# FNet layer with a gated feed-forward branch: the second sequence chunk of the first DFT changes from plain products to five plain and three seven-product steps, and the weight jobs move

## The chip, the cores and the metric

The program runs on one core of one Trainium2 chip. The metric is device time in microseconds (us) of one execution. Five engines work side by side: TensorE (PE in the profile, with its weight loads as PEld), VectorE (DVE), ScalarE (ACT), GpSimd (POOL) and SyncE (SP). SP issues nearly all DMA transfers of this kernel, one after the other from one queue. Each engine runs its own instructions strictly in the order in which the program holds them.

## The reference

All tensors are float32. S = 2048 tokens, D = 512, F = 1792.

```python
xn = layernorm(x)                                  # over D
a  = einsum("bsd,ed->bse", xn, dft_hid_re)
b  = einsum("bsd,ed->bse", xn, dft_hid_im)
s  = einsum("ts,bse->bte", dft_seq_re, a) - einsum("ts,bse->bte", dft_seq_im, b)
h  = einsum("bsd,df->bsf", xn, w1) + b1
h  = where(h > 0, h, 0) ** 2
g  = silu(einsum("bsf,fd->bsd", h, w2) + b2)
out = x + s * g
```

## The kernel before

Every float32 factor is split into a high part (rounded to TensorE's fp32r format) and a low part (the rest). A product then takes three passes: high by high, high by low, low by high. The high part is made on ACT (`split_hi`, profile line L136), the low part on DVE (`split_lo`, L139), which has to wait for ACT's part.

The largest stage multiplies the sequence DFT matrices by xn. It goes over eight chunks `c` of 256 columns of the DFT (`CW = 256`, `NC = 8`), and in each over eight pairs `j` of x row blocks (`NJ = 8`). A *step* (c, j) is one pair in one chunk. Two ways of multiplying occur:

- *Plain* (chunks 0 and 1 before, `products`, L397): a step takes 24 matmuls of 512 columns.
- *Seven products* (chunks 2 to 7, `mm`, L382): a 2x2 block product with seven instead of eight multiplications. A step takes 7 x 6 = 42 matmuls of 256 columns. It needs sums of the blocks on both sides: of x (`sums` and `split_sums`, `split_s1`, made once while the plain chunks run) and of the DFT columns (`step_sums(n+2)`, three DVE instructions, L304 to L306), and a split of seven blocks into the operand tile `g` (`step_split(n+1)`: ACT L136, then DVE L139, both on 128x1792). There are two `g` tiles in turn, so the split for step n+1 can start when TensorE has left step n-1, and has to be done when it starts step n+1. The DFT columns come as tile `u` (`load_c`, 512 KB, three or four steps ahead).

At the end of a seven-product chunk, seven sums of the seven accumulators make the four output blocks (`closing_of`, L363; ACT first copies some accumulators into tiles `left`). They are handed out over the first steps of the next chunk by the table `LATER = {0: 1, 1: 1, 2: 2, 4: 1}` (step: number of sums); two are made at once. After step max(LATER) the chunk is stored (`pqd<-c`, 1024 KB).

In between, the same engines prepare seven weight blocks for later stages, in *jobs*: `d0` to `d3` (hidden DFT matrices) and `v0`, `v1`, `v6` (three blocks of w1). A job (`weight`) loads a raw block of 512 KB (tile `wd2r` for `d2`, `w10r` for `v0` and so on), for the `d` jobs turns the sign of a part on ACT (L146), makes the sums on DVE (tile `wd2t`), splits first 768 and then 1024 columns (tile `wd2g`), and stores each split to memory (`wdd<-wd2g`, 768 and 1024 KB). It is a generator; the table `EARLY` says after which step which job does its next piece. In this kernel a job has four pieces: load; turn and sums; first split and store; second split and store. All jobs but `d1` share one raw buffer, so a job's load stands behind the previous job's splits.

The order of instructions on each engine is the order in which this Python code emits them; no scheduler moves them. In one turn of the loop over steps the order is: the step's matmuls, `step_sums(n+2)`, `step_split(n+1)`, the load of step n+4, the closing sums, then the pieces that `EARLY` names.

After that stage come the hidden DFT (`YUnit`, L790), the first feed-forward product (`HUnit`, L790) and the second one (`outer`, L896). For the units listed in `ACT_PAIR`, `HUnit` applies relu and square on ACT instead of DVE.

## Time and profile before

| | |
|---|---|
| median of 3 runs | 672.76 us (672.74 to 672.93) |
| the profiled execution's own time | 672.81 us |
| its span, first to last instruction | 671.0 us |
| PE busy | 665.1 us, 99% of the span |
| DVE busy | 596.4 us, 89% |
| ACT busy | 380.2 us, 57% |
| plain chunk 1 on PE (L397) | from 51.1 to 94.8 us |
| seven-product chunks 2 to 7 on PE (L382) | from 94.8 to 323.3 us |

Busy shares are averages over stages. The chain that ended last is PE for 96% of the span, so what counts is whether a stage makes PE wait, and how many columns PE has to stream. A duration of an instruction in the records runs a little into the next one; the distance from start to start is what it occupies its engine.

### The profile page before, as it was taken

To read this page: it belongs to the slowest core of one execution; us is meant where nothing else is said; L and a number is where in the kernel's file an instruction comes from. 1 tells how busy PE (TensorE), PEld (TensorE's weight loads), DVE (VectorE), ACT (ScalarE), POOL (GpSimd) and SP (SyncE) were. 2 spreads that over 40 slices of the span, in tenths; PEclk is the share of its full clock that TensorE was granted. 3 is DMA by queue.
4 is the path that set the end of the run, shared out by engine and by line. 5 is a ranking of instruction groups with operands and counts; after the bars stand their busy time and mean duration, and the time that the engine had idled before them with its cause. 6 is when DMAs were issued, how large, how long until landed. Compare 5 with 4: busy or idle time off the path is not lost.

```text
span 671.0 us, 13184 instructions
## 1 busy us (share of the span) xinstructions
PE 665.1 (99%) x5437; PEld 646.3 (96%) x5437; DVE 596.4 (89%) x831; ACT 380.2 (57%) x524; POOL 8.8 (1%) x11
## 2 busy tenths in 40 slices
PE   9999999999999999999999999999999999999997
PEld 6888889999999999999999999999999999999997
DVE  7997888999999999899899988977877889999997
ACT  6855664634445454444464557888778865454451
POOL 0000000000000000000000000000000000101010
PEclk9999999999999999999999999999999999999999
DMA  8635497646556774759588558565755866777775
GB/s 292 226 115 206 145 347 269 220 142 224 200 167 226 252 282 162 262 186 346 184 303 278 181 189 317 202 251 205 271 182 198 324 243 214 190 218 190 219 205 156
DMA packets 51739, 150.82 MB, mean 225 GB/s; under 512 B 4960, under 2 KB 19552, under 8 KB 50272
## 3 DMA queue, kind: packets, MB, share of 16 engines
q1 hardware_dynamic: 43568, 129.28, 56.9%
q10 hardware_dynamic: 6208, 18.88, 7.1%
q0 software_dynamic: 1904, 1.84, 1.9%
q8 instruction: 42, 0.69, 0.4%
q14 instruction: 17, 0.14, 0.1%
HBM read 101.98 MB, written 47.99 MB: 223 GB/s over the span
## 4 chain that ended last, share of the span: by engine, by line
PE 96%; DVE 1%; ACT 1%; DMA 0%; issue 0%; ACTq 0%; SPq 0%; DVEq 0%
PE m L382 34%; PE m_o L896 15%; PE r_B L790 13%; PE r_A L790 9%; PE pq_b L397 8%; PE r_C L790 4%; PE r_D L790 4%; PE m_last L896 4%; PE pq_ba L397 2%; PE pq_bc L397 2%; PE pq_bb L397 2%; DVE z L1146 0%; DMA x<-in_x 0%; DVE z L946 0%; ACT h L848 0%
## 5 line engine op out<-in xcount | busy, mean ns | idle before, releaser
L382 PEld LDWEIGHTS m<-g,xc 128*128 128x128 f32 x2016 | 228.6, 188 | 0.1
L382 PE MATMUL m<-g,xc 128*128 128x256 f32 x2016 | 228.7, 276 | 0.0
L136 ACT ACTIVATE g<-u 128x1792 fp32r<-128x1792 f32 (+2 forms) x65 | 99.0, 1523 | 126.9 <-PE m L382 89.0
L139 DVE TENSOR_TENSOR g<-u,g 128x1792 fp32r<-128x1792 f32 (+2 forms) x66 | 116.9, 1772 | 19.8 <-ACT g L136 19.2
L896 PE MATMUL m_o<-w,g 128*128 128x256 f32 x882 | 100.5, 276 | 0.0
L896 PEld LDWEIGHTS m_o<-w,g 128*128 128x128 f32 x882 | 100.3, 188 | 0.0
L136 ACT ACTIVATE g<-hr 128x1792 fp32r<-128x1792 f32 (+2 forms) x31 | 48.2, 1565 | 40.0 <-PE m_o L896 16.8
L790 PE MATMUL r_B<-xT,w 128*128 128x256 f32 x504 | 66.6, 277 | 0.4 <-ACT r_B L146 0.4
L397 PE MATMUL pq_b<-g,xc 128*128 128x512 f32 x240 | 65.2, 391 | 0.4 <-DVE small L247 0.4
L790 PEld LDWEIGHTS r_B<-xT,w 128*128 128x128 f32 x504 | 61.5, 188 | 0.5 <-ACT r_B L146 0.5
L139 DVE TENSOR_TENSOR g<-hr,g 128x1792 fp32r<-128x1792 f32 (+2 forms) x31 | 56.7, 1837 | 2.9 <-ACT g L136 2.8
L397 PEld LDWEIGHTS pq_b<-g,xc 128*128 128x128 f32 x240 | 44.7, 188 | 10.7 <-ACT g L136 0.8
L790 PE MATMUL r_A<-xT,w 128*128 128x256 f32 x336 | 42.8, 276 | 0.0
L790 PEld LDWEIGHTS r_A<-xT,w 128*128 128x128 f32 x336 | 40.2, 188 | 0.0
L790 PE MATMUL r_B<-wdp,yg 128*128 128x256 f32 x288 | 35.8, 277 | 0.0
L304 DVE TENSOR_TENSOR u<-u 128x512 f32<-128x512 f32 x48 | 32.8, 684 | 1.9 <-DMA u<-in_ct 1.9
L790 PEld LDWEIGHTS r_B<-wdp,yg 128*128 128x128 f32 x288 | 34.1, 188 | 0.0
L896 PE MATMUL m_last<-w,g 128*128 128x256 f32 x294 | 33.5, 276 | 0.0
L896 PEld LDWEIGHTS m_last<-w,g 128*128 128x128 f32 x294 | 33.4, 188 | 0.0
L139 DVE TENSOR_TENSOR yg<-yraw,yg 128x1792 fp32r<-128x1792 f32 x13 | 26.2, 2018 | 0.6 <-ACT yg L136 0.6
L136 ACT ACTIVATE yg<-yraw 128x1792 fp32r<-128x1792 f32 x13 | 22.2, 1708 | 5.8 <-DVE yraw L313 5.3
L790 PE MATMUL r_D<-xT,w 128*128 128x256 f32 x168 | 23.6, 276 | 0.0
(192 smaller groups left out, 877.8 us busy)
## 6 DMA issues: line engine op xcount, KB each, us to landing
u<-in_ct SPq DMA_DIRECT2D x63, 512.0 KB, 3.8
hd<-h ACTq DMA_DIRECT2D x28, 512.0 KB, 3.9
hr<-hd SPq DMA_DIRECT2D x28, 512.0 KB, 3.8
wdp<-wdd SPq DMA_DIRECT2D x8, 896.0 KB, 6.5
yraw<-pqd SPq DMA_DIRECT2D x13, 512.0 KB, 5.9
pqd<-c SPq DMA_DIRECT2D x6, 1024.0 KB, 6.3
w<-w1d SPq DMA_DIRECT2D x6, 896.0 KB, 8.2
y<-y ACTq DMA_DIRECT2D x8, 512.0 KB, 5.2
```

The lines of the kernel that those rows point to most:

```text
L136: nc.scalar.activation(hi, src, AF.Copy)
L139: nc.vector.tensor_tensor(lo, src, hi.bitcast(F32), op=ALU.subtract)
L304: nc.vector.tensor_tensor(t[:, 0:2], r[:, 0:1].to_broadcast([P, 2, 256]), r[:, 1:3], op=ALU.add)
L382: nc.tensor.matmul(ps[:, d], w[:, a_, d * P:(d + 1) * P], halves(mv(b_)), start=first and d == 0 and (a_, b_) == (HI, HI), stop=last and ( ...
L397: nc.tensor.matmul(accs[c][k], w, part[c, j][:, b_, 2 * h:2 * h + 2], start=j == 0 and h == 0 and (a_, b_) == (HI, HI), stop=j == NJ - 1 a ...
L790: nc.tensor.matmul(self.region(REGION[k]), w, mv, start=i == 0 and k in (1, 7), stop=i == len(ops) - 1, skip_group_check=True)
L896: nc.tensor.matmul(m[:, i * 256:(i + 1) * 256], ready[n][:, a_, H_SLOT[a], i * P:(i + 1) * P], W2[p][:, b_, b], start=p == 0 and i == 0 an ...
```

## The change

Chunk 1 is now multiplied in two ways. Five x pairs (`MIXED = 4, 5, 6, 7, 2`) are multiplied plainly, in matmuls of 256 columns, into four accumulators (`plain_step`); three of those accumulators are the ones that products 2, 3 and 4 of the seven use, the fourth is called Z. Then three pairs (`SEVEN = 1, 0, 3`) are multiplied by seven products into the same accumulators. The closing of chunk 1 therefore goes through `closing_of`, with one more DVE sum for Z. The sums of x no longer have a separate buffer for S1 (`split_s1` is gone; `split_sums` splits four blocks at once), and two of the eight `split_sums` come after the first seven-product step.

A weight job has five pieces instead of four: its first sum stands apart from the other two. `EARLY` is rewritten: `d0` begins in the plain steps and ends in the three seven-product steps, `d1` to `v6` follow in chunks 2 to 6 (`d1` used to be made in chunk 1 with a buffer of its own, and `d2` was begun there). In five places the last piece of a job and the load of the next job stand together, and the next job's second piece one step later. `LATER` hands out one closing sum per step. `ACT_PAIR` loses unit 5.

```diff
-PLAIN = 2
-SIDE = {7: 1}
+MIXED = 4, 5, 6, 7, 2
+SEVEN = 1, 0, 3
...
 EARLY = {
-    (2, 0): ("d2",), (2, 1): ("d2",), (2, 2): ("d3",), (2, 4): ("d3",), (2, 5): ("d3",), (2, 6): ("d3",),
-    (3, 1): ("v0",), (3, 3): ("v0",), (3, 5): ("v0",), (3, 6): ("v0",),
...
+    (1, 0): ("d0",), (1, 3): ("d0", "d1"), (2, 1): ("d1",), (2, 2): ("d1",), (2, 3): ("d1",), (2, 5): ("d1", "d2"),
+    (2, 6): ("d2",), (2, 7): ("d2",), (3, 1): ("d2",), (3, 3): ("d2", "d3"), (3, 4): ("d3",), (3, 5): ("d3",),
...
-LATER = {0: 1, 1: 1, 2: 2, 4: 1}
+LATER = {0: 1, 1: 1, 2: 1, 3: 1, 4: 1}
+LATER_1 = {0: 1, 1: 1, 2: 1, 3: 1, 4: 1, 5: 1}
...
-ACT_PAIR = (4, 5, 6, 8, 10, 12, 14, 16, 18, 21, 25)
+ACT_PAIR = (4, 6, 8, 10, 12, 14, 16, 18, 21, 25)
...
+    def plain_step(j):
+        g = part.pop((1, j))
+        for k, pairs_ in ((2, ((A11, 1), (A12, 3))), (4, ((A21, 1), (A22, 3))), (3, ((A11, 0), (A12, 2))),
+                          (Z, ((A21, 0), (A22, 2)))):
...
+            for i, (a, q) in enumerate(pairs_):
+                mm(ms[k], XC[j][:, a], lambda b_: g[:, b_, q], ...)
...
-    steps = [(c, j) for c in range(PLAIN, NC) for j in range(NJ)]
+    steps = [(1, j) for j in SEVEN] + [(c, j) for c in range(2, NC) for j in range(NJ)]
...
-    def weight(n, raw_, sums_, to, k, e=None, turn=False):
+    def weight(n, raw_, sums_, to, k, turn=False):
...
-        sums_(t, r)
+        first = sums_(t, r)
+        next(first)
+        yield
+        list(first)
         yield
...
+        if n == 0:
+            split_sums(2)
+            split_sums(7)
```

How the order of instructions moves, at two places. Numbers behind a name tell instances apart (`g3_0` is the operand of step (3, 0), `u3_1` the columns of step (3, 1), `wd1g` the split weights of job `d1`).

SP, the queue of DMA issues, around the load of one raw weight block. Before, at the load for `d3`:

```order
L432 DMA wdd2_85<-wd2g_939 256x1x768
L293 DMA u2_5_991<-in_ct 128x1024
L432 DMA wdd2_85<-wd2g_939 256x1x1024
L293 DMA u2_6_1044<-in_ct 128x1024
L423 DMA wd3r_1046<-in_wd 128x1024
L293 DMA u2_7_1097<-in_ct 128x1024
```

Now, at the load for `d2`, after step (2, 5):

```order
L286 DMA u3_1_1361<-in_ct 128x1024
L660 DMA pqd1_76<-c1_916 128x2048
L450 DMA wdd1_84<-wd1g_1253 256x1x1024
L438 DMA wd2r_1368<-in_wd 128x1024
L286 DMA u3_2_1419<-in_ct 128x1024
```

The raw block's load stood one step behind the last store of the job before, with a column load between; now it stands directly behind that store and, here, behind the store of a whole chunk.

DVE, after step (2, 5). Before, with the job `d3` at its sums and first split:

```order
L304 TENSOR_TENSOR wd3t_1047<-wd3r_1046 128x512
L305 TENSOR_TENSOR wd3t_1047<-wd3t_1047,wd3r_1046 128x256
L306 TENSOR_TENSOR wd3t_1047<-wd3t_1047,wd3r_1046 128x256
L304 TENSOR_TENSOR u2_7_1097<-u2_7_1097 128x512
L305 TENSOR_TENSOR u2_7_1097<-u2_7_1097 128x256
L306 TENSOR_TENSOR u2_7_1097<-u2_7_1097 128x256
L139 TENSOR_TENSOR g2_6_1203<-u2_6_1044,g2_6_1203 128x1792
L139 TENSOR_TENSOR wd3g_1208<-wd3r_1046,wd3g_1208 128x768
```

Now:

```order
L139 TENSOR_TENSOR g2_6_1358<-u2_6_1197,g2_6_1358 128x1792
L373 TENSOR_TENSOR c1_916<-m4_1_580,c1_916 128x2x256
L139 TENSOR_TENSOR wd1g_1253<-wd1t_1036,wd1g_1253 128x1024
L300 TENSOR_TENSOR u3_0_1305<-u3_0_1305 128x512
L302 TENSOR_TENSOR u3_0_1305<-u3_0_1305 128x256
L303 TENSOR_TENSOR u3_0_1305<-u3_0_1305 128x256
L139 TENSOR_TENSOR g2_7_1416<-u2_7_1250,g2_7_1416 128x1792
L300 TENSOR_TENSOR wd2t_1369<-wd2r_1368 128x512
L300 TENSOR_TENSOR u3_1_1361<-u3_1_1361 128x512
L302 TENSOR_TENSOR u3_1_1361<-u3_1_1361 128x256
L303 TENSOR_TENSOR u3_1_1361<-u3_1_1361 128x256
L139 TENSOR_TENSOR g3_0_1468<-u3_0_1305,g3_0_1468 128x1792
```

Between the end of one job (`wd1g`) and the first sum of the next (`wd2t`), which needs the load above, one column sum and one `g` split are left. On ACT the sign turn of `wd2r` stands between the high parts of `g2_7` and `g3_0` in the same way.

## Prediction

> **What bounds the kernel now.** First the page's engine rows and the clock row, then the chain of waits and the busy time by stage.

> ```profile
> PE 665.1 (99%) x5437; PEld 646.3 (96%) x5437; DVE 596.4 (89%) x831; ACT 380.2 (57%) x524; POOL 8.8 (1%) x11
> PEclk9999999999999999999999999999999999999999
> ```

> TensorE (PE) is busy all the time at full clock. Two things can change the total: the number of columns PE streams, and idle time that PE does not have today. The chain's pieces price a column:

> ```profile
> 56.56 2.04 PE pq_b L397 x9
> 58.60 0.68 PE pq_ba L397 x3
> ...
> 94.13 0.70 PE pq_ba L397 x3
> 94.83 228.49 PE m L382 x2016
> ```

> A 512-column matmul of plain chunk 1 takes 2.04 / 9 = 0.2267 us, a 256-column one of the seven products 228.49 / 2016 = 0.11334 us: half, to the nanosecond. Shorter matmuls cost nothing extra. A seven-product step is 42 x 0.11334 = 4.76 us; chunk 2's steps start at 94.83, 99.59, 104.35 and so on.

> By stage (columns: sum, busy time of PE, PEld, DVE, ACT, POOL, clock, DMA share, GB/s):

> ```profile
> 51.10:94.80 43.70, 43.70 (x195) 36.03 (x194) 36.84 (x47) 25.62 (x37) 0.00 (x0) 1.00 0.63 230
> 94.80:132.90 38.10, 38.10 (x339) 38.10 (x338) 34.55 (x44) 20.29 (x18) 0.00 (x0) 1.00 0.70 247
> 132.90:171.00 38.10, 38.10 (x339) 38.10 (x338) 35.40 (x45) 17.61 (x14) 0.00 (x0) 1.00 0.57 202
> ```

> PE never waits here, but in chunks 2 and 3 DVE is busy 34.6 and 35.4 of 38.1 us. So the question is how far DVE runs ahead of PE.

> **How much room a step has.** The timeline of ACT, then DVE, in chunk 2 (start, duration):

> ```profile
> 99.69 1.71 ACT L136 ACTIVATE g<-u 128x1792 fp32r<-128x1792 f32 x1 [1.79 <-issue]
> 115.58 0.61 ACT L146 ACTIVATE wd3r<-wd3r 128x512 f32<-128x512 f32 x1
> ...
> 101.43 2.03 DVE L139 TENSOR_TENSOR g<-u,g 128x1792 fp32r<-128x1792 f32 x1 [0.30 <-ACT g L136]
> 103.37 1.22 DVE L139 TENSOR_TENSOR wd2g<-wd2t,wd2g 128x1024 fp32r<-128x1024 f32 x1
> 104.51 0.69 DVE L304 TENSOR_TENSOR u<-u 128x512 f32<-128x512 f32 x1
> 105.23 0.42 DVE L305 TENSOR_TENSOR u<-u 128x256 f32<-128x256 f32 x1
> 105.69 0.43 DVE L306 TENSOR_TENSOR u<-u 128x256 f32<-128x256 f32 x1
> 106.19 2.02 DVE L139 TENSOR_TENSOR g<-u,g 128x1792 fp32r<-128x1792 f32 x1
> ...
> 194.03 0.68 DVE L363 TENSOR_TENSOR c<-m,c 128x512 f32<-128x512 f32 x1
> 194.63 0.68 DVE L304 TENSOR_TENSOR u<-u 128x512 f32<-128x512 f32 x1
> ```

> PE starts a step at 99.59. ACT's high part starts 0.10 later, DVE's low part at +1.84, and it ends at +3.87, while PE needs it at +4.76 (its first matmul, 0.11 us, takes the high parts alone). So DVE can be late by 1.0 us and no more. From start to start a low part occupies DVE 1.94 us, a closing sum 0.60, the 1024-column weight split 1.14, three column sums 1.52 (0.72, 0.46, and 0.43 less an overlap of 0.09).

> **The change, part by part.**

> *Columns.* A plain step keeps its columns (24 x 512 = 48 x 256); in three steps 48 matmuls become 42. Saved: 3 x 6 x 0.11334 = **2.04 us**. Chunk 1 also ran 43.72 us (51.11 to 94.83) against 192 x 0.2267 = 43.53, slower only near its end (the 0.70 row): 0.19 more. The shorter ACT_PAIR takes work off ACT in the feed-forward units, where PE has this one wait for ACT; at most it gives all of it back, at least nothing:

> ```profile
> PE r_B L790 <- ACT r_B L146: 0.4, 1, 0.4
> ```

> Together −2.6 us.

> *DVE in the three seven-product steps.* In steps (1, 1) and (1, 0) DVE has, between two low parts, two `split_sums` of 1024 columns (1.14 each, like the weight split) and three column sums: 1.14 + 1.14 + 1.52 + 1.94 = 5.74 against 4.76. At the turn to chunk 2 it has two closing sums, a 1024-column weight split and three column sums: 1.20 + 1.14 + 1.52 + 1.94 = 5.80, and the split has to wait for ACT. Followed through the order row by row, DVE enters step (1, 1) with its margin spent on the plain steps' work, and each of the three excesses falls on PE: 0.96 us each, **+2.9 us**. Bounds: if it enters with its 1.0 us of margin and ACT costs nothing, 1.9; if ACT's part of a split, 1.71 us for the largest, comes wholly in the way once, 4.6.

> *The weight loads: the large term.* Five times (after (2, 5), (3, 3), (4, 0), (4, 5), (5, 3)) the next raw block is loaded right behind the previous job's last store, and its sums are due one step later; before, two steps lay between. Let T be PE's start of step (2, 5). DVE's low part of g(2, 6) runs T+1.84 to T+3.78, then a closing sum to T+4.38, then the weight split, which ends at T+5.60. Only then SP issues the store, and 0.5 us later the load, at about T+6.15. On ACT the sign turn stands before the high part of g(3, 0); on DVE the first sum stands before that low part. PE needs g(3, 0) at T + 3 x 4.76 + 0.11 = T+14.39. After the landing come the turn 0.61, the first sum 0.60 (512 columns, like a closing sum), three column sums 1.52, the low part 2.02: 4.75 us. So the block may land at T+9.64, **3.5 us after its issue**; for `v` jobs, which have no turn, 4.1 us. All later time is idle time of PE, one for one.

> How long do such loads take? Issues of the trace (KB each, us from issue to landing; first all seven raw loads, then the stores of 1024 KB):

> ```profile
> wd0r<-in_wd SPq DMA_DIRECT2D x1, 512.0 KB, 4.6
> wd1rt<-in_wd SPq DMA_DIRECT2D x1, 512.0 KB, 5.4
> wd2r<-in_wd SPq DMA_DIRECT2D x1, 512.0 KB, 4.9
> wd3r<-in_wd SPq DMA_DIRECT2D x1, 512.0 KB, 4.8
> w10r<-in_w SPq DMA_DIRECT2D x1, 512.0 KB, 4.3
> w11r<-in_w SPq DMA_DIRECT2D x1, 512.0 KB, 4.6
> w16r<-in_w SPq DMA_DIRECT2D x1, 512.0 KB, 5.6
> ...
> wdd<-wd1g SPq DMA_DIRECT2D x1, 1024.0 KB, 4.7
> wdd<-wd3g SPq DMA_DIRECT2D x1, 1024.0 KB, 6.8
> w1d<-w10g SPq DMA_DIRECT2D x1, 1024.0 KB, 5.4
> pqd<-c SPq DMA_DIRECT2D x6, 1024.0 KB, 6.3
> u<-in_ct SPq DMA_DIRECT2D x1, 512.0 KB, 9.1
> ```

> None of the seven landed within 4.1 us, though no store stood right ahead of any. The last row is the `u` issued at 80.74, behind a load pair and two weight stores begun at 77.99:

> ```profile
> 77.99 0.33 SPq L423 DMA_DIRECT2D wd2r<-in_wd  x1
> 80.74 0.56 SPq L293 DMA_DIRECT2D u<-in_ct  x1
> 80.00:90.00 10.00, 10.00 (x45) 8.26 (x44) 8.30 (x15) 4.70 (x7) 0.00 (x0) 1.00 1.00 371
> ```

> It waited its turn behind all of them: 512 + 512 + 768 + 1024 + 512 = 3328 KB from 77.99 to 89.84, 11.85 us, with the DMA engines full at 371 GB/s. From this:

> - After (3, 3), (4, 0), (5, 3): a 1024 KB store directly ahead. It lands 4.7 to 6.8 us after its issue, say 5.8; the load is issued 0.5 later and needs 512 KB at 371 GB/s, 1.4 us, more: 6.7 us. PE idles 6.7 − 3.5 = 3.2, then 2.6 and 2.6: **8.4 us**.
> - After (2, 5), (4, 5): column load, chunk store, weight store, raw load, 3072 KB within about 2.2 us. By the measured case 11.85 x 3072 / 3328 = 10.9 after the first issue, 8.7 after the load's own. PE idles 5.2 and 4.6; and in the step after it DVE has two closing sums, the two remaining weight sums (0.80, like the two column sums from 105.23), column sums and low part: 1.20 + 0.80 + 1.52 + 1.94 = 5.46 against 4.76, 0.7 more each time: **11.2 us**.

> Bounds of the five: if the store ahead costs nothing and each lands in the median 4.8 us, 1.3 + 0.7 + 0.7 + 2.0 + 1.4 = 6.1; if the store takes its longest 6.8 and the 9.1 us of the full queue holds with 1 us on top, about 25. I take 19.6: the queue of issues is the same as in the measured row.

> Nothing after chunk 6 moves enough to count: the last job ends at (6, 0), its copies are read chunks later.

> **Sum.** −2.6 + 2.9 + 19.6 = +19.9. The profiled execution took 672.81 (span 671.0 and 1.8 around it), 0.05 above the median of 672.76; the forecast is 692.7 us, **slower by 3%**.

> **Rivals.** Under 0.2% (1.35 us) no measurement of this kernel tells a difference.

> 1. *Loads land as quickly as before.* If stores and loads share the engines so that the load does not wait for the store, the five cost 6.1 as bounded above: 672.8 − 2.6 + 2.9 + 6.1 = 679. For it: `wd2r` landed in 4.9 us with 2816 KB issued behind it. Against it: the 9.1 us row, where the late one paid. Chance 0.14.
> 2. *Faster.* The one point that decides is whether the raw blocks land within 3.5 and 4.1 us. Then the five waits vanish; with 1.9 for the DVE excess it would end at 672.1, with the excess hidden in DVE's margin too at 670.2. Column loads do land that fast, but none of the seven raw loads did:

> ```profile
> u<-in_ct SPq DMA_DIRECT2D x63, 512.0 KB, 3.8
> ```

> Chance 0.02 for faster, 0.03 for no change.
> 3. *PE loses its clock in the long waits.* The two longest waits leave PE idle for 4 to 5 us at a stretch. A slow start shows what a lower rate costs:

> ```profile
> 1.22 5.46 PE L503 MATMUL warm<-idle 128*128 128x512 bf16 x13 [1.22 <-DVE idle L499]
> ```

> 13 warm-up matmuls took 0.42 us each, where warm ones take 0.227. One such stretch loses 13 x 0.193 = 2.5 us; after two long waits 5.0, so 697.7. DVE would catch up meanwhile, so this is an upper price. [...] Chance 0.13, since the idle time is cut by matmuls on the high parts alone.

> The rest, 0.68, is the forecast with its own range of 687 to 698. The range of 684 to 700 takes in most of the clock's case and the upper part of the quick loads. Slower 0.95, same 0.03, faster 0.02.

> **What would show it.** On PE, the first product of g(3, 0) (chunk 3's `m`) waiting 4 to 6 us, for ACT or DVE, the same at (5, 0), and 2 to 3 us before (3, 6), (4, 3), (5, 6); ACT's turn of `wd2r` waiting for the DMA `wd2r<-in_wd`, with a landing near 9 us; raw loads at 6 to 10 us where they were 4.3 to 5.6; DVE waits about 1 us short at PE in the steps (1, 0), (1, 3) and (2, 1). Chunk 1 should end near 94.7, no earlier than now by more than 0.5, its saved columns eaten by DVE. The forecast is wrong if those raw loads land in under 4.1 us, or if PE waits mainly in stages after chunk 6.

## The result, and the profile after

The changed kernel takes **705.75 us** (median of 4 runs, 704.02 to 710.22) beside 672.85 us (672.74 to 673.15) for the kernel before: a ratio of 1.050, interval 1.045 to 1.055. It is slower by 33 us. The forecast was 692.7 us with a range of 684 to 700: the sign and the places were right, the size was 13 us too small, and the result lies above the range. The profiled execution took 704.48 us, with a span of 702.7.

The engine rows, the clock row and the first line of the chain, from the page of the changed kernel:

```profile
PE 675.6 (96%) x5611; PEld 662.1 (94%) x5611; DVE 606.6 (86%) x841; ACT 380.6 (54%) x516; POOL 8.8 (1%) x11
PEclk9999999989999999999999999999999999999999
PE 69%; DVE 18%; DMA 7%; ACT 3%; issue 1%; SPq 1%; ACTq 0%; DVEq 0%
```

The chain was 96% PE before. Now it leaves PE for DVE, DMA and ACT, and one slice of the clock row shows less than full speed. The waits of PE say where (us in total, times, longest):

```profile
PE m L388 <- DVE g L139: 14.8, 8, 3.9
PE m L388 <- ACT c L146: 4.3, 1, 4.3
...
PE r_B L799 <- ACT r_B L146: 1.2, 1, 1.2
```

By stage (the columns are those of the table of before: length, busy time of PE, PEld, DVE, ACT, POOL, clock, DMA share, GB/s), cut at the ends of chunk 1, of step (2, 6), of step (5, 7) and of chunk 7:

```profile
50.93:94.69 43.76, 42.57 (x367) 42.08 (x366) 37.35 (x42) 24.63 (x28) 0.00 (x0) 1.00 0.40 138
94.69:129.25 34.56, 33.79 (x296) 33.59 (x295) 32.72 (x42) 15.19 (x12) 0.00 (x0) 1.00 0.60 204
129.25:276.36 147.11, 129.44 (x1052) 127.95 (x1051) 115.22 (x147) 59.76 (x52) 0.00 (x0) 0.94 0.58 204
276.36:353.20 76.84, 76.84 (x676) 76.79 (x675) 66.33 (x82) 33.23 (x27) 0.00 (x0) 1.00 0.70 248
```

Chunk 1 ends at 94.69, where the first product of chunk 2 starts (94.67 before; the 94.83 of the chain of before is the recorded end of chunk 1's last product, which runs a little into the next one): DVE took the saved columns back. The third row is where the time went: 25 steps of 4.76 us make 119.0 us, and they took 147.11, with a mean clock of 0.94. Chunk 7 ends at 353.20, 29.9 us later than before, and what follows it takes 349.5 us against 347.7.

That the raw blocks are what is waited for is seen in the timeline of ACT and DVE ahead of step (3, 0) (the bracket is the idle time before, and what ended it):

```profile
135.76 0.63 ACT L146 ACTIVATE wd2r<-wd2r 128x512 f32<-128x512 f32 x1 [9.31 <-DMA wd2r<-in_wd]
...
136.42 0.69 DVE L300 TENSOR_TENSOR wd2t<-wd2r 128x512 f32<-128x512 f32 x1 [7.49 <-ACT wd2r L146]
```

The DMA issues of the five blocks (KB, us from issue to landing):

```profile
wd2r<-in_wd SPq DMA_DIRECT2D x1, 512.0 KB, 9.7
wd3r<-in_wd SPq DMA_DIRECT2D x1, 512.0 KB, 6.3
w10r<-in_w SPq DMA_DIRECT2D x1, 512.0 KB, 6.6
w11r<-in_w SPq DMA_DIRECT2D x1, 512.0 KB, 7.2
w16r<-in_w SPq DMA_DIRECT2D x1, 512.0 KB, 6.6
```

DVE stands still for 7.5 us, since the first sum of the weight job is the next instruction of its queue. The column sums of `u` behind it could have run: their columns had landed at 128.26.

### The profile page after: what moved, and what is told of

The parts are those of the page before. It is cut to its first block, busy times and chain, and to the rows that moved or that the text cites. A ratio compares the mean times of both kernels' runs of the same rounds, so it can differ in the third digit from the quotient of the medians.

```text
span 702.7 us, 13529 instructions
## 1 busy us (share of the span) xinstructions
PE 675.6 (96%) x5611; PEld 662.1 (94%) x5611; DVE 606.6 (86%) x841; ACT 380.6 (54%) x516; POOL 8.8 (1%) x11
## 3 DMA queue, kind: packets, MB, share of 16 engines
q0 software_dynamic: 1904, 1.84, 1.9%
## 4 chain that ended last, share of the span: by engine, by line
PE 69%; DVE 18%; DMA 7%; ACT 3%; issue 1%; SPq 1%; ACTq 0%; DVEq 0%
PE m L388 21%; PE m_o L905 14%; PE r_B L799 12%; PE r_A L799 8%; DVE g L139 7%; PE pq_b L399 5%; PE r_C L799 4%; PE r_D L799 4%; ACT g L136 2%; PE pq_bb L399 2%; DVE c L373 1%; DMA wd2r<-in_wd 1%; DVE u L300 1%; DMA pqd<-c 1%; DMA w11r<-in_w 1%
## 5 line engine op out<-in xcount | busy, mean ns | idle before, releaser
L388 PE MATMUL m<-g,xc 128*128 128x256 f32 x2382 | 282.6, 282 | 19.6 <-DVE g L139 14.8
L388 PEld LDWEIGHTS m<-g,xc 128*128 128x128 f32 x2382 | 280.4, 192 | 21.9 <-DVE g L139 16.5
L136 ACT ACTIVATE g<-u 128x1792 fp32r<-128x1792 f32 (+2 forms) x65 | 100.8, 1551 | 145.3 <-PE m L388 85.7
L139 DVE TENSOR_TENSOR g<-u,g 128x1792 fp32r<-128x1792 f32 (+2 forms) x66 | 119.2, 1807 | 16.9 <-ACT g L136 16.8
L136 ACT ACTIVATE g<-hr 128x1792 fp32r<-128x1792 f32 (+2 forms) x31 | 48.2, 1566 | 39.9 <-PE m_o L905 16.8
L139 DVE TENSOR_TENSOR g<-hr,g 128x1792 fp32r<-128x1792 f32 (+2 forms) x31 | 56.7, 1838 | 2.9 <-ACT g L136 2.8
L399 PE MATMUL pq_b<-g,xc 128*128 128x512 f32 x144 | 40.9, 391 | 0.8 <-ACT g L136 0.8
L300 DVE TENSOR_TENSOR u<-u 128x512 f32<-128x512 f32 x51 | 34.9, 684 | 1.3 <-DMA u<-in_ct 1.2
L399 PEld LDWEIGHTS pq_b<-g,xc 128*128 128x128 f32 x144 | 26.8, 188 | 7.0 <-ACT g L136 1.2
L139 DVE TENSOR_TENSOR yg<-yraw,yg 128x1792 fp32r<-128x1792 f32 x13 | 26.2, 2018 | 0.8 <-ACT yg L136 0.8
L136 ACT ACTIVATE yg<-yraw 128x1792 fp32r<-128x1792 f32 x13 | 22.2, 1710 | 8.0 <-DVE yraw L314 7.5
L799 PE MATMUL r_C<-xT,w 128*128 128x256 f32 x168 | 23.7, 277 | 0.0
## 6 DMA issues: line engine op xcount, KB each, us to landing
u<-in_ct SPq DMA_DIRECT2D x63, 512.0 KB, 3.6
hd<-h ACTq DMA_DIRECT2D x28, 512.0 KB, 4.2
hr<-hd SPq DMA_DIRECT2D x28, 512.0 KB, 3.7
pqd<-c SPq DMA_DIRECT2D x7, 1024.0 KB, 6.5
yraw<-pqd SPq DMA_DIRECT2D x13, 512.0 KB, 5.1
y<-y ACTq DMA_DIRECT2D x8, 512.0 KB, 4.8
```

The lines of the kernel that those rows point to most:

```text
L136: nc.scalar.activation(hi, src, AF.Copy)
L139: nc.vector.tensor_tensor(lo, src, hi.bitcast(F32), op=ALU.subtract)
L300: nc.vector.tensor_tensor(t[:, 0:2], r[:, 0:1].to_broadcast([P, 2, 256]), r[:, 1:3], op=ALU.add)
L388: nc.tensor.matmul(ps[:, d], w[:, a_, d * P:(d + 1) * P], halves(mv(b_)), start=first and d == 0 and (a_, b_) == (HI, HI), stop=last and ( ...
L399: nc.tensor.matmul(accs[k], w, part[0, j][:, b_, 2 * h:2 * h + 2], start=j == 0 and h == 0 and (a_, b_) == (HI, HI), stop=j == NJ - 1 and ...
L799: nc.tensor.matmul(self.region(REGION[k]), w, mv, start=i == 0 and k in (1, 7), stop=i == len(ops) - 1, skip_group_check=True)
```

## The experiments

### The five loads and the chunk's store

*Loads early.* Each of the five loads is issued at the previous job's first store instead of behind its last one; nothing else is changed.

```diff
-    ... (2, 3): ("d1",), (2, 5): ("d1", "d2"), ... (3, 1): ("d2",), (3, 3): ("d2", "d3"), ...
+    ... (2, 3): ("d1", "d2"), (2, 5): ("d1",), ... (3, 1): ("d2", "d3"), (3, 3): ("d2",), ...
```

> The changed kernel with one thing moved: each of the five raw weight loads that stood right behind the previous job's last store is issued at that job's first store instead, one or two steps earlier. Theory (the five landings cost 19.6 us of waiting, and the half clock is their consequence): the five waits and every half-clock stretch go; what stays is DVE's 3.5 us in the three seven-product steps and some 1.5 us in the first feed-forward units, against 2.6 us saved: 672.85 - 2.6 + 5.0 = 675, range 673.5 to 677. Rival (DVE simply has more work than fits the steps, the landing is only the last thing to come): DVE stays late in the same steps and it takes 690 or more. Rival (loads land slowly wherever they are issued in this table): waits of 1 to 3 us remain, 680 to 688.

Measured: 679.63 us, ratio to the kernel before 1.0097 (1.0083 to 1.0111). Its waits of PE in this stage:

```profile
PE m L388 <- DVE g L139: 2.9, 5, 0.8
```

Who waited for the line that issues the raw loads, and how long these took:

```profile
  ACT wd1r L146: 2.3, 1
...
DMA to landing us min/median/max: 5.6/5.9/7.4
```

The loads are hardly quicker (median 5.9 us, 6.6 in the changed kernel), but nobody is waiting for the five any more, and 26 of the 33 us are gone. The two rivals fall. The time is 4.6 us above the expectation and outside its range. DVE accounts for 1.6 us of that: with the waits gone it has no pause to catch up, and steps (3, 1) and (5, 1) take 0.6 and 1.0 us longer too. In the profiled execution another 0.8 us was lost before chunk 1 began, 0.7 us in steps that ran slower without a wait of PE, and 0.7 us more than expected after chunk 7; the rest stays open.

*And the store early.* In addition, the results of chunks 2 to 6 are stored after the fifth step again.

```diff
-            if j == max(LATER_1):
+            if j == max(LATER_1 if c == 2 else LATER):
```

> The kernel with the early loads, and a chunk's result stored after the fifth step of the next chunk again (as in the kernel before) for all chunks but the first of the two mixed ones. Theory (the store one step later keeps ACT from the last chunk's result, and that is the 1.2 us wait of r_B): that wait and ACT's wait for the DMA pqd<-c near the end of chunk 7 go; the time falls by up to 1 us against the early loads alone, or not at all where a wait of DVE in chunk 5 takes its place: 673.5 to 675.5. Rival (the r_B wait comes from ACT's own load of work, ACT_PAIR or the order of copies): the wait stays at 1 us or more and the time is that of the early loads.

Measured: 678.17 us, 1.0069 (1.0057 to 1.0082): 1.5 us less than with the early loads alone, but above the range, as that kernel was. No `r_B` wait is left. In the changed kernel's timeline the store of chunk 6 on SP and ACT's copy of the next result into the same tile stand like this:

```profile
343.16 0.47 SPq L660 DMA_DIRECT2D pqd<-c  x1
...
352.25 0.60 ACT L146 ACTIVATE c<-m 128x512 f32<-128x512 f32 x1 [5.83 <-DMA pqd<-c]
```

The store landed 9.0 us after its issue, at 352.17, 1.0 us before chunk 7 ended; ACT had stood still for it and made its copies late. In the kernel before, the store was issued at 309.44 and landed at 317.49, before the last step of chunk 7 began (318.40), and ACT made the same copy 0.9 us into that step, waiting only for PE:

```profile
319.28 0.60 ACT L146 ACTIVATE c<-m 128x512 f32<-128x512 f32 x1 [2.46 <-PE m L382]
```

So the 1.2 us wait of `r_B` came from the late store. After the end of chunk 7 the kernel with early loads alone took 349.8 us, this one 347.4, before it was 347.7. DVE is late in chunk 5 by 0.8 us at (5, 0) and at (5, 1), where it was 1.0 us at (5, 1) alone; that took back part of it, as expected.

### The same pattern in the kernel before

Three loads of the kernel before are put right behind the last store of the job ahead, due one step later; for that, the last pieces of three jobs move too. Column count, DVE's work and the closing sums are those of before.

```diff
-    ... (2, 6): ("d3",), (3, 1): ("v0",), ...
+    ... (3, 2): ("d3", "v0"), ...
```

> The kernel BEFORE, with the changed kernel's pattern for three loads alone: the raw blocks of v0, v1 and v6 are loaded right behind the previous job's last store and due one step later; everything else, the column count and DVE's work too, is that of before. Theory (glued loads are the cause by themselves): three waits of PE of about 3.6 us each, +10.8, and up to 1.7 us more for each that trips the half clock: 683.5 to 689. Rival (they cost only together with the changed kernel's fuller DVE steps): 673 to 676. Rival (loads land in the 4.3 to 5.6 us of before even here): three waits under 1.5 us, 674 to 677.

Measured: 688.04 us, 1.0217 (1.0202 to 1.0231). Who waited for the loads:

```profile
  DVE w16t L310: 3.3, 1
  DVE w11t L310: 3.3, 1
  DVE w10t L310: 3.2, 1
...
DMA to landing us min/median/max: 4.8/5.7/6.1
```

Three times DVE waits 3.2 to 3.3 us, PE for 9.8 us in all, and the kernel is 15 us slower. In the kernel before itself nobody waits for any of these loads. So the pattern alone is enough; the fuller DVE steps of the change aren't needed for it.

### What the lost clock costs

In chunks 1 to 7 the changed kernel's trace has four stretches at clock 0.50, one of 6.83 us and three of 3.41. The forecast had priced two at 2.5 us and given them a chance of 0.13 only. The four start at 138.56, 176.11, 203.41 and 234.13: 37.55, 27.30 and 30.72 us apart, which is 11, 8 and 9 times 3.413 us (95.57 us in all, over 28). The stretches of 3.413 us that this divides the trace into are called *windows* below. First, empty products (zero operand, into an accumulator that they leave as it is) were put into the five waits:

```diff
+        for i in range(FILL.get(s, 0)):
+            nc.tensor.matmul(m[:, 0:256], XC[0][:, 0, HI, 0:P], <zeros>, ...)
```

> The changed kernel with 125 empty products (0.113 us each, zero operand, accumulating nothing) ahead of the five first products that wait: 34 at (3, 0), 20 at (3, 6), 20 at (4, 3), 31 at (5, 0), 20 at (5, 6). The loads land as late as before, so the sum of waiting is the same, but PE is busy in it. Theory (the waits trip the clock to half, and that costs 7.8 us on top of the 19.6 of the waits): no half-clock stretch, chunk 7 ends 7 to 9 us earlier, 695 to 700. Rival (the half clock overlaps time in which DVE would be late anyway and costs nothing): 703 to 707 with full clock in the records. Rival (the empty products delay the real ones): above 706.

Measured: 705.05 us, no gain: a miss. One half-clock stretch was left, and `w11r` landed 10.2 us after its issue (7.2 in the changed kernel). Next, the same in the kernel before with three late loads:

> The kernel before with three late loads (688.04 us: three waits of 3.2 to 3.3 us, two of them followed by 3.41 us at half clock), and 27 empty products (3.06 us) put into each of the three waits. The loads land no sooner. Theory (a stretch at half clock costs its 1.7 us on top of the wait, and the slower products after it 0.2 us a step): no half-clock stretch, 688.0 - 2 x 1.71 - 4 x 0.19 = 683.9, range 683 to 685. Rival (the slow stretch costs nothing, since the data come late anyway): 687 to 688.5.

Measured: 686.74 us, 1.0201 (1.0187 to 1.0215), so 1.3 us less than without filling, between the two theories. No stretch at half clock was left, but DVE waited 3.2, 3.9 and 4.0 us for the loads where it had waited 3.2, 3.3 and 3.3. Landings vary by more than the effect sought, so neither run decides. The question was then asked without a transfer:

```diff
+            for _ in range(AGAIN.get(s, 0)):            # AGAIN = {(3, 5): 3, (4, 5): 3, (5, 5): 3}
+                split_lo(g[:, HI], g[:, LO], u[:, 1:8])
```

> The kernel before, with the low-part subtraction of g repeated three more times (1.94 us each, same result) at (3, 5), (4, 5) and (5, 5): DVE is late by a fixed amount and no transfer has a part in it. Each time PE waits 3 x 1.94 less at most 1.0 of margin, about 4.8 to 5.4 us, so at least one 3.413 us window is idle by more than half. Theory (the half clock is a cost of its own): 673.2 + 3 x 5.2 + 3 x 1.7 = 694, range 692 to 696, three half-clock stretches. Rival (no cost of its own): 688 to 690.

> The same three delays of DVE, and 44 empty products (4.99 us) put into each wait of PE. The data come as late as without them. Theory (the half clock is a cost of its own, and PE kept busy does not lose it): no half-clock stretch, 688 to 690, 4 to 6 us less than without the empty products. Rival (the slow stretch is hidden, since DVE has no margin after the wait): the same time within 1 us.

Measured side by side: **696.39 us** (1.0354, 1.0339 to 1.0369) without and **692.04 us** (1.0282, 1.0268 to 1.0296) with the empty products. DVE's delay is the same in both. Without filling, stretches of time at the first place (the product count stands behind PE's time, the clock is the third value from the end); the window ahead of 161.82, from 158.41, is wholly idle:

```profile
155.60:159.01 3.41, 1.26 (x12) 1.06 (x10) 3.34 (x3) 2.18 (x2) 0.00 (x0) 1.00 0.01 2
159.01:161.82 2.81, 0.00 (x0) 0.00 (x0) 2.77 (x2) 0.26 (x1) 0.00 (x0) 1.00 0.00 0
161.82:165.23 3.41, 2.93 (x13) 2.93 (x14) 3.34 (x6) 0.00 (x0) 0.00 (x0) 0.50 0.55 109
```

With filling PE is busy at that place and the clock stays at 1.00:

```profile
156.38:161.88 5.50, 5.50 (x52) 5.50 (x50) 5.40 (x4) 2.43 (x2) 0.00 (x0) 1.00 0.02 4
```

The lost clock costs 4.4 us for three waits, 5.2 by the spans (694.1 and 688.9): about 1.5 to 1.7 us a wait, on top of the wait. In the two profiled executions the three places differ by 1.5, 2.2 and 1.4 us; at the second the half clock lasted 6.83 us instead of 3.41. Another 0.8 us lies in the four steps after the first wait, which ran slower at full clock (see the last section). Both times are above their ranges, since each delay cost 5.7 us instead of 5.2. Back to the changed kernel, with longer filling:

> The changed kernel with longer runs of empty products: 52 at (3, 0), 26 at (3, 6), 26 at (4, 3), 45 at (5, 0), 26 at (5, 6), so that no window is idle by half. Theory A (the 1.7 us of each half-clock stretch come back): 697 to 700. Theory B, after the first try at 705.05 (where PE keeps its clock it reaches the next block sooner, and the loads are later for it by nearly as much): 702 to 706 with full clock throughout, and the landings of the raw blocks 7 to 10 us after their issue.

Measured: **701.45 us**, 1.0422 (1.0407 to 1.0436), 4.3 us below the changed kernel, with full clock throughout. Both theories have a part: 4.3 us come back, not 7. The five stretches with a late block, in the changed kernel (5, 2, 5, 3 and 2 steps, 80.92 us at full pace; the first one, and the sum of all five):

```profile
129.25:161.89 32.64, 26.76 (x212) 26.27 (x211) 23.19 (x31) 12.53 (x12) 0.00 (x0) 0.90 0.43 158
...
sum 108.84, PE 91.17 PEld 89.68 DVE 80.03 ACT 39.63 POOL 0.00; mean PE 18.23 PEld 17.94 DVE 16.01 ACT 7.93 POOL 0.00
```

The same five with filling, first row and sum:

```profile
129.75:161.25 31.50, 30.92 (x264) 30.51 (x263) 23.29 (x31) 12.54 (x12) 0.00 (x0) 1.00 0.45 164
...
sum 104.90, PE 103.94 PEld 102.96 DVE 78.74 ACT 39.52 POOL 0.00; mean PE 20.79 PEld 20.59 DVE 15.75 ACT 7.90 POOL 0.00
```

They cost 27.9 us in the changed kernel and 24.0 us with the clock kept: 3.9 us less without the half clock; the rest is the blocks and, for 1.1 us, slower products.

*When is the clock lost?* In the kernel before with three late loads, the first wait (157.0 to 160.2) kept its clock and the second and third, as long, did not. Shifting all of it by 0.91 us asks why:

> The kernel before with three late loads, and 8 empty products (0.91 us) at (3, 0), far ahead of the waits. The wait at (3, 5) lay 48% in one 3.413 us window and 45% in the next (the windows counted from the starts of the half-clock stretches) and kept its clock. Theory (the clock halves after a window of 3.413 us that is idle by more than half): shifted by 0.91 it lies 0.7 in one window and is followed by a half-clock stretch that it did not have; the time is 688.0 + 0.9 + 1.7 = 690.7, or about 689 if the wait at (4, 5) comes to lie across two windows in turn. Rival (the first wait is spared because it is the first, or because of its length): (3, 5) stays at full clock, 689.

Measured: 691.90 us (689.55 to 695.08). All three waits now lose the clock; the theory held. Unshifted, the two windows around the first wait (idle for 48% and 45%), and the one before the second (75%):

```profile
155.24:158.66 3.42, 1.78 (x16) 1.58 (x14) 3.28 (x7) 0.28 (x1) 0.00 (x0) 1.00 0.12 47
158.66:162.07 3.41, 1.87 (x16) 1.88 (x17) 3.34 (x5) 2.15 (x2) 0.00 (x0) 1.00 0.24 44
...
199.62:203.03 3.41, 0.84 (x7) 0.84 (x8) 3.38 (x5) 2.43 (x2) 0.00 (x0) 1.00 0.00 0
203.03:206.44 3.41, 3.41 (x19) 3.41 (x18) 3.34 (x5) 0.00 (x0) 0.00 (x0) 0.50 0.82 269
```

Shifted, at the first wait (the row begins 0.09 us into the window, which is idle for 84%):

```profile
159.01:162.33 3.32, 0.55 (x4) 0.55 (x5) 3.29 (x5) 2.37 (x2) 0.00 (x0) 1.00 0.01 2
162.33:165.74 3.41, 3.41 (x18) 3.41 (x17) 3.34 (x5) 0.06 (x1) 0.00 (x0) 0.50 0.87 250
```

### The shorter ACT_PAIR alone

> The kernel before with the shorter ACT_PAIR alone. Theory: the 0.4 us wait of r_B for ACT goes, 672.6 to 672.8 against 673.05 (a gain near what can be measured). Rival (the wait moves to another unit): 673.0 or above.

Measured: 672.83 us beside 673.40, ratio 0.9995 (0.9987 to 1.0004). The wait of `r_B` is gone from the list of waits; its 0.4 us is too small for this measurement to tell.

### A version without the three causes

The pieces of the jobs were dealt out anew: every load two to four steps ahead of its first use, nothing at the turn of a chunk, sums and splits of the plain steps a step earlier.

> The changed kernel with all three causes taken away: loads go two to four steps ahead of their first use, chunk results are stored a step earlier, and the weight jobs' pieces are dealt out so that no step of DVE goes over its margin: column sums with three of the side sums and the splits of the plain steps a step earlier, d0's splits at (1, 0) and (2, 1), no piece at a turn of chunks. The columns saved are the same. Theory (the idea of the change is sound, its table is not): no wait of PE in chunks 1 to 7 above 0.5 us, 673.05 - 2.04 - 0.2 - 0.3 = 670.5, range 669.5 to 672.5. Rival (mixing plain and seven-product steps costs more than its columns by itself): 673 or more without a wait to be seen.

Measured: 674.07 us, 1.0013 (1.0002 to 1.0023): a miss by 3.6 us. The profiled execution was the fastest of eleven, 672.61 us, so its trace shows only part of that. PE still waits once for ACT, 0.7 us at the start of step (3, 0). ACT's copy of a chunk's first result at the ends of chunks 2 and 3, from its timeline:

```profile
130.64 0.60 ACT L174 ACTIVATE c<-m 128x512 f32<-128x512 f32 x1 [3.00 <-PE m L416]
...
167.38 0.58 ACT L174 ACTIVATE c<-m 128x512 f32<-128x512 f32 x1
```

The second comes 1.8 us after the start of its step (3, 7), the first 5.0 us after the start of (2, 7). The profile names PE for the wait, but PE had long been done; the store of chunk 1 out of the same tile, issued at 121.49, landed at 130.56. That is the late store again: chunk 1 has eight closing sums, and they end one step later. Three more moves:

```diff
-LATER_1 = {0: 1, 1: 1, 2: 1, 3: 1, 4: 1, 5: 1}
+LATER_1 = {0: 1, 1: 1, 2: 1, 3: 1, 4: 2}
-    (2, 4): ("d1", "d2"), ... (6, 3): ("y1", "p0"), ...
+    (2, 5): ("d1", "d2"), ... (6, 3): ("p0",), (6, 5): ("y1",), ...
```

> The changed kernel with the jobs' pieces spread as in the run before it (674.07, where 2.4 us of waits were left at (2, 7), (3, 0) and (6, 5)), and three more moves: the closing sums of chunk 1 end one step sooner, so that its store lands before ACT writes the next result into the same tile; the blocks of d1 and d2 one step later; the early sums of y1 at (6, 5) instead of (6, 3). Theory: no wait above 0.4 us is left in chunks 1 to 7, 671 us, range 670.3 to 672, below the kernel before. Rival (new waits take their place, DVE being busy 35 of 38 us): 672.5 to 675.

Measured: **671.87 us** beside 672.89, ratio **0.9980 (0.9971 to 0.9989)**: a little faster than the kernel before, and 34 us faster than the changed one with the same columns. In chunks 1 to 7 its list of waits has no entry; by stage from chunk 1 on, to the end of chunk 3:

```profile
51.03:92.51 41.48, 41.48 (x367) 41.47 (x366) 37.26 (x42) 24.48 (x27) 0.00 (x0) 1.00 0.42 144
92.51:130.59 38.08, 38.08 (x338) 38.08 (x337) 36.78 (x48) 19.07 (x17) 0.00 (x0) 1.00 0.63 227
130.59:168.67 38.08, 37.93 (x333) 37.72 (x332) 36.54 (x48) 19.02 (x17) 0.00 (x0) 1.00 0.69 235
```

Chunk 1, from its first product to chunk 2's first, takes 41.5 us instead of 43.7: the 2.2 us of saved columns are there. In the profiled execution 0.8 us of them is lost again in chunks 3 and 5, and 0.8 us in the units after chunk 7. DVE is busy 36.8 of 38.1 us in chunk 2, which leaves little room; that this causes the losses was not tested.

## Why the prediction was right and wrong

Three terms make up most of the miss: the five loads (mis-sized), the half clock (left out of the likeliest sum) and the chunk's store (put at nothing). No one of them alone would have carried the time out of the range.

- *Columns, −2.2 us of chunk 1:* right, as the last version shows. In the changed kernel they are hidden by DVE.
- *ACT_PAIR, −0.4 us at most:* right in kind; too small to be seen in the time.
- *DVE in the seven-product steps, +2.9 us:* right in kind and 0.6 too small. Chunk 1 took 43.76 us where its products need 41.48, 2.3 us over; with 1.2 us in step (2, 1) it is 3.5. (The forecast's own sums, 5.74, 5.74 and 5.80 against 4.76, give 3.0, not 3 x 0.96.)
- *The five loads, +19.6 us:* the mechanism, all five places and the step where each falls were right, and four of the five landings were within about a microsecond: 9.7 us where 8.7 was forecast, 6.3 to 6.6 where 6.7 was. The fifth took 7.2 instead of 8.7, but the block was not there sooner, as SP needed 2.36 us to issue the store in front of it and issued the load at 221.97, 7.6 us after the step's start and not 6.15. PE's waits at the five places were 5.9, 2.7, 2.6, 3.9 and 2.6 us, 17.7 together; the forecast had 5.2, 3.2, 2.6, 4.6 and 2.6, 18.2 together. But the term was mis-sized: with the clock kept the five cost 24.0 us. 2.1 of the missing 4.4 are the two landings behind the chunk's store, about 1 us later in that run than forecast; about 1.1 are products that run a little slower after a wait (below); 1.2 stay open.
- *The clock:* this is the step whose mechanism failed. The forecast put it at nothing in the likeliest sum and made it a rival of chance 0.13, for the two longest waits only, "since the idle time is cut by matmuls on the high parts alone". That reason did not hold: four of the five waits lost the clock, two of 2.6 and 2.7 us among them (another of 2.6 us kept it), and the price was about 4 us in all (4.3 by the times of the two kernels, 3.9 by the five stretches). No run shows the rival's 5.0 us, 2.5 a wait: they were the author's estimate, taken from the 13 slow products at the start (0.42 us each), and the trace of before, with a mean granted clock of 1.000, has no slow stretch after a wait. What the runs showed in its place are stretches of 3.41 us at 0.50, one of 6.83, at about 1.5 to 1.7 us a wait, and a window idle for 58% was followed by one (172.69 to 176.11).
- *"Nothing after chunk 6 moves enough to count":* wrong. The store of a chunk one step later, which `max(LATER_1) = 5` brings to all chunks, was counted in the forecast only as one more transfer ahead of two of the loads. The tile it holds is the one that ACT needs at the end of the chunk. It cost 2.2 us in the units after chunk 7 (349.5 us against 347.7, less the 0.4 us expected).

Together: 0.6 for DVE, 4.0 for the clock, 4.9 for the late blocks and slower products (0.5 of it after the five stretches), 2.2 for the store, 11.7 of the 11.8 us by which the span exceeds the forecast.

## What to carry to other kernels

When a load moves directly behind a store in the same queue, price it from a row where a load stood behind stores (the five here landed after 6.3 to 9.7 us, the seven raw loads of before after 4.3 to 5.6), and ask which engine has its first use next: there, the whole queue stops, as DVE's did here for 7.5 us. Put a price for lost clock on each wait of TensorE of 2.6 us or more in the likeliest case: of the 14 such waits in the four unfilled kernels with late data (the changed one, and the one before with three late loads, with those shifted, and with three delays of DVE), 12 lost the clock, and the three of the last cost about 1.5 us each on top. When a table sets the last step of anything, look up what its buffer is needed for next.

## What the runs showed of the hardware

```profile
264.85:268.27 3.42, 1.79 (x15) 1.79 (x16) 3.35 (x5) 2.24 (x2) 0.00 (x0) 1.00 0.25 46
...
138.46:141.87 3.41, 1.68 (x12) 1.48 (x13) 3.41 (x5) 2.97 (x4) 0.00 (x0) 1.00 0.06 14
141.87:145.28 3.41, 3.41 (x19) 3.41 (x18) 3.31 (x6) 0.00 (x0) 0.00 (x0) 0.50 0.38 144
...
172.69:176.11 3.42, 1.45 (x12) 1.45 (x13) 3.35 (x5) 2.43 (x2) 0.00 (x0) 1.00 0.24 14
176.11:179.52 3.41, 3.41 (x18) 3.41 (x18) 3.38 (x4) 0.00 (x0) 0.00 (x0) 0.50 0.85 324
```

It was the position in the window, not the length of the wait, that decided between equal waits: in the changed kernel the one of 2.60 us that ended at 202.97 lay within one window and lost the clock; the one of 2.58 us that ended at 266.48 lay across two, idle for 28% and 48%, and kept it. The stretches at 0.50 lasted 3.41 us, or 6.83 us where PE was idle in the first window of the two for 45% (at 138.56 in the changed kernel) and 62% (at 206.20 with three delays of DVE: 2.11 us idle in all, counted to the first window), while 14% at 161.82 there was followed by full clock. In the windows shown that were busy throughout, 18 or 19 products were counted at 0.50 and 30 to 32 at full clock.

After some waits, products ran at full granted clock but started 117.8 ns apart instead of 113.3, for a few steps: 42 products took 4.95 us in the first row and 4.76 in the second, both of the changed kernel. DVE's and the DMA engines' load didn't tell the two kinds apart here (slow steps had DMA shares from 0.21 to 0.94 and 3.4 to 4.9 us of DVE; the fast one below had 0.62 and 4.1). What causes it stays open.

```profile
209.44:214.39 4.95, 4.95 (x45) 4.95 (x43) 3.39 (x4) 2.44 (x2) 0.00 (x0) 1.00 0.21 84
...
286.26:291.02 4.76, 4.76 (x45) 4.76 (x43) 4.08 (x6) 1.71 (x1) 0.00 (x0) 1.00 0.62 220
```
